# Additive attention masks of the first batch: four 64 by 64 array tiles in place of full matmuls, in an attention and MLP-mixer kernel

## The chip, the cores and the metric

The kernel runs on one core of a Trainium2 chip. The metric is the device time of one execution in microseconds; several executions are timed, and one more is profiled. The core's engines appear in the profile as PE (TensorE; its weight loads are PEld), DVE (VectorE), ACT (ScalarE), POOL (GpSimd) and SP, which here only issues DMAs.

## The reference

Four batches of 768 rows go through windowed attention with sink columns (8 heads of width 64), and the result, 512 wide, through a mixer: a token MLP over the rows, a residual, and a channel MLP with a residual.

```
scores = scale * q @ k.T                      # per batch and head, 768 x 768
keep   = (column < 4) | (0 <= row - column < 128)
a      = softmax(where(keep, scores, -1e9))
x      = a @ v                                # heads side by side: 768 x 512
u      = x + (relu(x.T @ w_tok1) @ w_tok2).T  # w_tok1 768 x 256
out    = u + relu(u @ w_ch1) @ w_ch2          # w_ch1 512 x 1536
```

Only two diagonals of 128 x 128 blocks of the scores matter, and the four sink columns.

## The kernel before

The heads are taken two at a time: 16 pairs, four for each batch, with head i of a pair in rows 64i to 64i+63 of the transposed q and k. The work falls into a first stage and a long rest.

*First attention* (`first_attention`, batch 0, pairs 0 to 3). SP loads q and k of the four pairs in float32 (`load_raw`, line 81); an engine casts each to bf16 (`cast`: ACT for pair 0's q, POOL for pair 3, DVE for the others). `turn` transposes a pair's q or k on TensorE by 64-row halves against `ident` (line 442) and the results are copied out as qT and kT, in two parts each. The scores come in three groups g for each pair: 512, 512 and 384 columns for each head, both heads in one PSUM tile `ps_sc` of two slots, one half of the tile for each head. `scores` (matmuls of 64 rows by 128 columns, the heads in the two row halves) adds to what `masked` has put there: -32768 where a score is masked out. `masked` writes that with a matmul of the identity by the mask, 128 rows by 128 columns, one for each head. ACT then takes the exponential (line 509) straight out of PSUM. Eleven of the twelve groups are masked this way (`MASKED_BY_PE`); the one of pair 3, group 0 is masked by a multiplication on DVE. `score_sinks` does the sink columns for two pairs, `pv` the product with v, with `recip` and `norm` on DVE behind it. The values v come by POOL's DMAs with a cast (`load_v`, line 102), the first four rows of v for the sinks by four small SP loads (line 188) into `v_sink_f`, which DVE has set to zero before, and which POOL casts to `v_sink`. POOL's list has then v of pairs 1 and 2, `w_tok1` (line 127), v of pair 3, and so on.

*The rest*: the token mixing (`mix_h` with w_tok1, `mix_u` with w_tok2), the attention of batches 1 to 3, where no mask is added by TensorE, and the channel MLP (`mix_channels`, lines 849 to 940), which is most of TensorE's work.

*The order.* Until line 200 or so each engine's instructions stand in the order in which the program names them. From there `Plan.run` makes the order: it goes through units of TensorE work and the operations of the other engines behind them, with a cost in nanoseconds for each, and gives the next place to what can begin first by its own reckoning. A unit marked `half` is one that works on 64-row halves; between a `half` unit and another it reckons `SWITCH` (95), and from the first attention's units it prefers one of the same kind. So a unit's cost and its mark change the order of all that comes later, on every engine. The order, once made, is fixed in the program.

At the start of the program DVE has this list: `ones`, zeros in `mask_add`, six memsets of the ones columns of `v_aug` (line 169), zeros in `kTs` (182) and `v_sink_f` (184), four small memsets (192), and then what the plan gives it, the cast of pair 0's k first. POOL makes `ident`, cuts `mask_add` with two affine selects (159, 163) and sets its sink rows to zero (167).

Of the kernel before, what the change touches and what calls it, by code (L numbers as in the profile page):

```python
# [10 lines left out]
BF16 = mybir.dt.bfloat16  # L11
# [5 lines left out]
def kernel(  # L17
# [13 lines left out]
    nc = tc.nc  # L31
    B, H, S, D = q.shape
    P = 128
# [15 lines left out]
    singles = ctx.enter_context(tc.tile_pool(name="singles", bufs=1))  # L49
# [13 lines left out]
    def bank(tag, *shape, dtype=FP32, slot=None):  # L63

        n = given[tag].pop(0) if slot is None else slot
        return psum.tile([P, *shape], dtype, name=f"ps_{tag}", tag=f"{tag}{n}", bufs=1)

    in_order = tc.keep_in_program_order
# [39 lines left out]
    def mm(*args, **kwargs):  # L108
        in_order(nc.tensor.matmul(*args, skip_group_check=True, **kwargs))  # L109
# [19 lines left out]
    done = {}  # L129
# [8 lines left out]
    def keep_warm(n, slot):  # L138
# [12 lines left out]
    mask_add = singles.tile([P, 4, 2, P], BF16)  # L151
    mask_adds = [mask_add[:, ts(n, 2)] for n in range(2)]
    in_order(nc.vector.memset(mask_add, 0.0))
    ident = singles.tile([P, P], BF16)
    in_order(nc.gpsimd.memset(ident, 0.0))
    in_order(nc.gpsimd.affine_select(
        out=ident, in_=ident, compare_op=ALU.not_equal, fill=1.0, base=0, pattern=[[-1, P]], channel_multiplier=1,
    ))
    in_order(nc.gpsimd.affine_select(
        out=mask_add[:, :, 0], in_=mask_add[:, :, 0], compare_op=ALU.is_ge,  # L160
# [3 lines left out]
        out=mask_add[:, :, 1], in_=mask_add[:, :, 1], compare_op=ALU.is_ge,  # L164
        fill=MASKED, base=-1, pattern=[[0, 4], [-1, P]], channel_multiplier=1,
    ))
    in_order(nc.gpsimd.memset(mask_add[0:n_sink, 2], 0.0))
    for n in range(NV):
        in_order(nc.vector.memset(v_buf[n][:, :, :, D:D1], 1.0))

# [14 lines left out]
    for n in range(4):  # L185
        i, odd = n // 2, n % 2
        rows = slice(D * i + ODD * odd, D * i + ODD * odd + n_sink)
        in_order(nc.sync.dma_start(  # L188
            out=v_sink_f[rows, odd::2, i, 0:D],
            in_=v[0].rearrange("(p o i) s d -> i o s p d", i=2, o=2)[i, odd, 0:n_sink],  # L190
# [166 lines left out]
    def unit(ns, fn, deps=(), need=None, then=(), half=False):  # L357

        op = Op({"PE": float(ns)}, fn, deps, then, size=float(ns))
        for f in then:  # L360
            if op not in f.deps:
                f.deps.append(op)
        op.need = need or {}
        op.half = half
        return op
# [102 lines left out]
    def width(g):  # L468
        return 3 * P if g == NT // 2 - 1 else 4 * P

    def masked(p, g):

        def run():
            ps = tiles["ps_s", p, g] = bank("sc", 2, 4 * P)
            for i in range(2):
                mm(
                    ps[:, i, 0:width(g)], ident,
                    mask_adds[g == 0].rearrange("p k n q -> p (k n q)")[:, 0:width(g)], start=True, stop=False,
                )

        x = done["exp", p, g] = Op({}, None)
        deps = [done["tk", 0]] if p == 0 else []
        done["mask", p, g] = unit(width(g) * 0.84, run, deps, {"sc": [[x]]})
        return done["mask", p, g]

    def scores(p, g):
# [295 lines left out]
    def first_attention():  # L782

        for p in range(NHP):
            prepare(p)
        turned = [turn(p, n) for p in range(NHP) for n in range(2)]
        masks, scored, out = [], [], []
        for p in range(NHP):
            for g in range(NT // 2):
                if (p, g) in MASKED_BY_PE:  # L790
                    masks.append(masked(p, g))
                scored.append(burst(scores(p, g)))
                if g == 0 and p == NHP - 1:
                    scored.append(score_sinks(p))
            if p == 1:
                out.append(score_sinks(p))
            if p % 2:
                out += [pv(n, half) for n in (p - 1, p) for half in range(2)]
        tokens = []
        for g in range(2):  # L800
            tokens.append([mix_h(0, g, t, 1) for t in range(NTOK)])
            tokens[g] += [mix_u(0, g, st, 2, g == 0 or st == 2) for st in range(0, NT, 2)]
            tokens[g] += [transpose_u(0, g, st, 2) for st in range(0, NT, 2)]
        return scored, masks, turned, out, *tokens[::-1]
# [265 lines left out]
```

## Time and profile before

| | us |
|---|---|
| median of 3 runs | 209.58 |
| lowest and highest | 209.21, 210.65 |
| the profiled execution's own time | 209.46 |
| its span, first instruction to last | 207.7 |

The span is what the profile's times are counted in; 1.76 us lie around it. The granted clock of TensorE was 0.998 over the span. Busy shares of the span: PE 95%, PEld 57%, DVE 55%, ACT 55%, POOL 32%. A matmul's time in the profile goes from its start to its modelled end, so that one that follows closely on another overlaps it: the distance between starts, not the duration, is what one more matmul costs.

The matmuls of `masked` are the rows `ps_sc<-mask_add,ident`: twelve of 512 and eight of 384 columns were recorded (the program has fourteen and eight), from 6.7 to 20.8 us after the start.

### The profile page before, as it was taken

Reading aid. Unit: us, or ns where it says so; the run is one execution under the profiler, and the core shown is the slowest. Engines: PE = TensorE matmul, PEld = TensorE weight load, DVE = VectorE, ACT = ScalarE, POOL = GpSimd, SP = SyncE. Lnnn points to the kernel's source line nnn. Section 1 sums busy time; section 2 is a strip of 40 time slices with the busy share of each in tenths; the row PEclk is TensorE's granted clock in tenths of the full one; section 3 lists DMA queues with packets and bytes.
Section 4 is the critical chain, followed back from the end, with each engine's and each line's share of the span. In section 5 each row is a group of like instructions: output and inputs, shape, how many; then the busy total and the mean of one; then the engine's idle time right before and its main releaser. Section 6 shows DMA issues by size and latency. Waiting matters only on the chain.

```text
span 207.7 us, 5034 instructions
## 1 busy us (share of the span) xinstructions
PE 198.0 (95%) x2126; PEld 119.3 (57%) x2145; DVE 114.3 (55%) x252; ACT 114.4 (55%) x202; POOL 67.5 (32%) x86
## 2 busy tenths in 40 slices
PE   6699999999999999999999999999999999999994
PEld 2345975566665665557656645666666445665443
DVE  4786664777577675867576552767674421000222
ACT  4799668878727435867684241868751103774000
POOL 6399759794699980720000000000000000000000
PEclk9999999999999999999999999999999999999999
DMA  6999999999999999795000212100001122000222
GB/s 198 283 260 182 172 174 191 156 164 201 156 159 176 185 206 195 52 70 37 3 0 5 101 51 104 51 5 0 3 0 49 56 101 101 3 0 0 101 104 101
DMA packets 73222, 21.57 MB, mean 104 GB/s; under 512 B 63216, under 2 KB 70256, under 8 KB 73200
## 3 DMA queue, kind: packets, MB, share of 16 engines
q0 software_dynamic: 67232, 11.80, 71.9%
q1 hardware_dynamic: 5968, 9.45, 12.9%
q8 instruction: 17, 0.28, 0.6%
q14 instruction: 5, 0.04, 0.1%
HBM read 26.75 MB, written 6.29 MB: 159 GB/s over the span
## 4 chain that ended last, share of the span: by engine, by line
PE 83%; DMA 6%; DVE 4%; ACT 2%; issue 2%; POOL 1%; SPq 0%; POOLq 0%; DVEq 0%
PE ps_mx L109 75%; PE ps_sc L109 5%; DMA w_tok<-in_moe_w_tok_dram 4%; DMA v_sink_f<-in_v_dram 2%; PE ps_sc L460 2%; DVE x_sb L615 1%; ACT qT L116 1%; DVE kT L118 1%; POOL v_aug L102 1%; PE ps_mx L745 1%; ACT v1T L122 1%; DVE recip L612 1%; PE ps_mx L112 1%; POOL v_sink L118 0%; SPq L188 0%
## 5 line engine op out<-in xcount | busy, mean ns | idle before, releaser
L109 PE MATMUL ps_mx<-uT,w_ch 128*128 128x384 bf16 x384 | 68.3, 326 | 0.9 <-DVE x_sb L615 0.9
L109 PE MATMUL ps_mx<-w_ch,v1T 128*128 128x512 bf16 (+2 forms) x299 | 64.2, 362 | 0.9 <-issue 0.3
L122 ACT ACTIVATE v1T<-ps_mx 128x384 bf16<-128x384 f32 x74 | 36.3, 493 | 33.7 <-PE ps_mx L109 22.9
L109 PEld LDWEIGHTS <-w_ch 128*128 128x128 bf16 x384 | 35.5, 98 | 25.0 <-DVE x_sb L615 2.5
L109 PEld LDWEIGHTS <-v1T 128*128 128x128 bf16 x312 | 28.9, 98 | 29.2
L509 ACT ACTIVATE pT<-ps_sc 128x1024 bf16<-128x1024 f32 (+1 forms) x48 | 44.4, 956 | 2.2 <-PE ps_sc L109 1.9
L884 DVE TENSOR_TENSOR o_sb<-ps_mx,u_sb 128x512 f32<-128x512 f32 x23 | 15.9, 691 | 44.6 <-PE ps_mx L109 44.6
L94 POOL DMA_DIRECT2D q_bf<-in_q_dram x24 | 19.7, 822 | 4.7 <-DMA w_ch<-in_moe_w_ch_dram 2.4
L109 PEld LDWEIGHTS <-w_tok 128*128 128x128 bf16 x192 | 18.3, 98 | 4.8 <-DMA w_tok<-in_moe_w_tok_dram 0.5
L94 POOL DMA_DIRECT2D k_bf<-in_k_dram x24 | 19.6, 820 | 3.1 <-DMA w_ch<-in_moe_w_ch_dram 1.7
L102 POOL DMA_DIRECT2D v_aug<-in_v_dram x16 | 16.4, 1028 | 10.9 <-PE ps_mx L109 8.0
L118 DVE COPY kT<-ps_sc 128x768 bf16<-128x768 bf16 x11 | 10.5, 958 | 17.0 <-ACT qT L116 17.0
L516 DVE TENSOR_TENSOR pT<-pT,mask_main 128x1024 bf16<-128x1024 bf16 (+1 forms) x24 | 14.5, 620 | 3.6 <-ACT pT L509 3.5
L109 PE MATMUL ps_sc<-qT,kT 64*128 64x256 bf16 x192 | 15.5, 262 | 0.3
L109 PE MATMUL ps_mx<-v_aug,pT 128*128 128x65 bf16 x352 | 15.3, 194 | 0.0
L716 DVE TENSOR_TENSOR u_sb<-ps_mx,x_sb 128x512 bf16<-128x512 f32 x20 | 12.7, 685 | 4.2 <-PE ps_mx L109 4.2
L109 PEld LDWEIGHTS <-pT 128*128 128x128 bf16 x352 | 13.5, 97 | 2.0 <-issue 0.6
L124 DVE TENSOR_SCALAR v1T<-ps_mx 128x384 bf16<-128x384 f32 x22 | 12.1, 554 | 2.7 <-PE ps_mx L109 2.0
L109 PE MATMUL ps_mx<-h1T,w_tok 128*128 128x256 bf16 x96 | 12.6, 273 | 0.0
L116 ACT ACTIVATE qT<-ps_sc 128x768 bf16<-128x768 bf16 x11 | 8.9, 810 | 6.4 <-PE ps_sc L460 6.2
L109 PE MATMUL ps_mx<-x_sb,w_tok 128*128 128x256 bf16 x96 | 12.0, 273 | 0.1
L615 DVE TENSOR_TENSOR x_sb<-ps_mx,recip 128x384 bf16<-128x384 f32 x22 | 11.4, 551 | 0.1
(72 smaller groups left out, 152.2 us busy)
## 6 DMA issues: line engine op xcount, KB each, us to landing
out_dram<-o_sb SPq DMA_DIRECT2D x23, 256.0 KB, 2.0
v_aug<-in_v_dram POOLq DMA_DIRECT2D x16, 192.0 KB, 6.5
w_ch<-in_moe_w_ch_dram POOLq DMA_DIRECT2D x8, 384.0 KB, 8.9
q_bf<-in_q_dram POOLq DMA_DIRECT2D x24, 96.0 KB, 6.6
k_bf<-in_k_dram POOLq DMA_DIRECT2D x24, 96.0 KB, 5.6
q_f<-in_q_dram SPq DMA_DIRECT2D x4, 384.0 KB, 5.6
k_f<-in_k_dram SPq DMA_DIRECT2D x4, 384.0 KB, 5.9
w_tok<-in_moe_w_tok_dram POOLq DMA_DIRECT2D x2, 384.0 KB, 8.1
```

The costliest lines, as they stand in the source:

```text
L94: in_order(nc.gpsimd.dma_start(out=out[:, h], in_=rows[:, h]))
L102: in_order(nc.gpsimd.dma_start(out=v_aug.rearrange("p i t d -> p (i t) d")[:, :, 0:D], in_=v[b].rearrange("h s d -> (h s) d")[2 * hp * S:2 ...
L109: in_order(nc.tensor.matmul(*args, skip_group_check=True, **kwargs))
L116: in_order(nc.scalar.activation(out, in_, AF.Copy))
L118: in_order({"DVE": nc.vector, "POOL": nc.gpsimd}[e].tensor_copy(out=out, in_=in_))
L122: in_order(nc.scalar.activation(out, in_, AF.Relu))
L124: in_order(nc.vector.tensor_scalar_max(out=out, in0=in_, scalar1=0.0))
L509: in_order(nc.scalar.activation(part(tiles["pT", p][:, :, ds(2 * g, 2)]), tiles["ps_s", p, g][:, :, 0:width(g)], AF.Exp, scale=scale,))
L516: in_order(nc.vector.tensor_tensor(out=pt, in0=pt, in1=m, op=ALU.mult))
L615: in_order(nc.vector.tensor_tensor(out=x_sb[b][:, :, ds((2 * hp + i) * D, D)], in0=tiles["ps_o", p, i][:, :, 0:D], in1=tiles["recip", p, i ...
L716: in_order(nc.vector.tensor_tensor(out=u_part(b, g, s0, n), in0=tiles["ps_u", b, g, s0], in1=x_sb[b][:, s0:s0 + n, c0:c0 + cn], op=ALU.add,))
L884: in_order(nc.vector.tensor_tensor(out=o_sb.rearrange("p (g c) -> p g c", g=2), in1=u_rows(b, st), in0=tiles["ps_out", b, st].rearrange("p ...
```

## The change

A second copy of the additive masks, `mask_swap`, is made by two DVE copies of 64 rows by 1024 columns: the lower 64 rows hold the upper 64 rows of `mask_add` and the other way round. The copies stand in the program right behind the masks' last step and ahead of the memsets of `v_aug`, `kTs` and `v_sink_f`.

`masked` now issues four matmuls for each group in place of two. Each takes 64 rows of a mask and the 64 by 64 corner of the identity that belongs to these rows, and writes 64 partitions of one head's half of `ps_sc`:

| matmul | rows read | mask | partitions written | head's half |
|---|---|---|---|---|
| i=0, x=0 | 0-63 | mask_add | 0-63 | 0 |
| i=0, x=1 | 64-127 | mask_add | 64-127 | 0 |
| i=1, x=0 | 0-63 | mask_swap | 64-127 | 1 |
| i=1, x=1 | 64-127 | mask_swap | 0-63 | 1 |

The unit's reckoned cost goes from 0.84 to 0.44 ns a column, and it gets the mark `half`.

```diff
     in_order(nc.gpsimd.memset(mask_add[0:n_sink, 2], 0.0))
+    mask_swap = singles.tile([P, 4, 2, P], BF16)
+    for x in range(2):
+        in_order(nc.vector.tensor_copy(out=mask_swap[ds(D * x, D)], in_=mask_add[ds(D * (1 - x), D)]))
     for n in range(NV):
         in_order(nc.vector.memset(v_buf[n][:, :, :, D:D1], 1.0))
...
         def run():
             ps = tiles["ps_s", p, g] = bank("sc", 2, 4 * P)
             for i in range(2):
-                mm(
-                    ps[:, i, 0:width(g)], ident,
-                    mask_adds[g == 0].rearrange("p k n q -> p (k n q)")[:, 0:width(g)], start=True, stop=False,
-                )
+                m = (mask_add, mask_swap)[i][:, ts(int(g == 0), 2)].rearrange("p k n q -> p (k n q)")
+                for x in range(2):
+                    rows = ds(D * x, D)
+                    mm(
+                        ps[ds(D * (x ^ i), D), i, 0:width(g)], ident[rows, rows], m[rows, 0:width(g)],
+                        start=True, stop=False,
+                    )
 
         x = done["exp", p, g] = Op({}, None)
         deps = [done["tk", 0]] if p == 0 else []
-        done["mask", p, g] = unit(width(g) * 0.84, run, deps, {"sc": [[x]]})
+        done["mask", p, g] = unit(width(g) * 0.44, run, deps, {"sc": [[x]]}, half=True)
```

In the order that the plan makes of it, every engine's list differs from about the first scores on: in the first stage ACT gets two pairs of the small kTs copies in place of two kT copies, and DVE the other way round; the mask and scores of pair 3, group 1 stand ahead of the first `mix_h`. SP's and POOL's lists keep their order.

## The prediction

> **What bounds the kernel now.** I read the page's slices first, then the chain that ended last, then the waits and the timeline of the first 28 us, the only stretch with the lines that the diff touches.
>
> ```profile
> PE   6699999999999999999999999999999999999994
> ...
> ACT  4799668878727435867684241868751103774000
> ...
> DMA  6999999999999999795000212100001122000222
> ...
> PE 83%; DMA 6%; DVE 4%; ACT 2%; issue 2%; POOL 1%; SPq 0%; POOLq 0%; DVEq 0%
> ```
>
> A slice is 5.2 us. After the first two or three, TensorE is full to the end: a microsecond taken off the start should come off the whole. The chain says what the start is made of:
>
> ```profile
> 2.58 0.50 DVE v_sink_f L184
> ...
> 4.12 4.17 DMA v_sink_f<-in_v_dram
> ...
> 8.46 0.92 POOL v_sink L118
> 9.38 1.95 POOL v_aug L102 x2
> 11.33 7.89 DMA w_tok<-in_moe_w_tok_dram
> ...
> 19.27 0.83 PE ps_mx L109 x6
> 20.10 1.25 PE ps_sc L109 x12
> 21.34 5.84 PE ps_mx L109 x88
> ```
>
> Up to 19.27 us the chain is no mask at all: a DVE memset, four tiny loads of the sink rows, a cast and two loads on POOL, and the landing of w_tok1, which TensorE's first token-mixing matmul waits for. From there TensorE itself carries it. The masks' part in it is within "ps_sc x12" at 20.10.
>
> Beside that chain, ScalarE was full from 8 to 20 us. The waits of the first 30 us (engine, line, releaser, total, times, longest) hold two waits of its exponentials:
>
> ```profile
> ACT pT L509 <- PE ps_sc L109: 1.1, 2, 0.7
> ...
> PE ps_sc L109 <- ACT pT L509: 0.9, 2, 0.5
> ```
>
> ```profile
> 10.00:15.00 5.00, 4.53 (x74) 2.32 (x72) 4.36 (x11) 4.97 (x9) 5.00 (x7) 1.00 1.73 278
> 15.00:20.00 5.00, 4.69 (x78) 2.94 (x80) 3.42 (x10) 4.78 (x8) 5.00 (x7) 1.00 1.65 186
> ```
>
> Columns after the length: busy PE, weight loads, DVE, ACT, POOL, then granted clock (1.00), DMA, GB/s. From 10 to 20 us ACT is at 9.75 of 10, PE at 9.2. So a shorter mask there mostly buys TensorE time to wait for ScalarE. The two places where TensorE kept ScalarE waiting are here (start, length, engine, line):
>
> ```profile
> 5.78 0.56 DVE L118 CAST k_bf<-k_f 128x768 bf16<-128x768 f32 x1 [2.29 <-DMA k_f<-in_k_dram]
> ...
> 6.68 1.04 PE L109 MATMUL ps_sc<-mask_add,ident 128*128 128x512 bf16 x4
> 6.78 0.87 ACT L116 ACTIVATE kT<-ps_mx 128x384 bf16<-128x384 bf16 x2 [0.62 <-PE ps_mx L442]
> ...
> 7.65 0.61 PE L109 MATMUL ps_sc<-qT,kT 64*128 64x256 bf16 x8
> ...
> 8.08 1.02 ACT L509 ACTIVATE pT<-ps_sc 128x1024 bf16<-128x1024 f32 x1 [0.43 <-PE ps_sc L109]
> ```
>
> ```profile
> 19.93 0.92 PE L109 MATMUL ps_sc<-mask_add,ident 128*128 128x512 bf16 x4
> ...
> 21.22 1.73 ACT L509 ACTIVATE pT<-ps_sc 128x1024 bf16<-128x1024 f32 x2 [0.66 <-PE ps_sc L109]
> ```
>
> At 6.68 four masks stand ahead of the first scores; the first half of kT is out at about 7.27 (half of 0.87 after 6.78, and 0.05), the scores begin at 7.65. At 19.93 four more stand ahead of the last two score groups.
>
> **The change, part by part.** *Masks.* Eleven groups, 7 of 512 columns and 4 of 384. Four 512 masks took 1.04 us, of which about 0.17 is the tail of the last (a lone one is 0.38): 0.216 each, so 0.162 for 384. Before: 14 x 0.216 + 8 x 0.162 = 4.3 us. After there are 44 matmuls of 64 rows by 64 columns. No row shows such tiles. Nearest are the scores, 64 rows by 128 columns: 8 of 256 in 0.61 us is (0.61 - 0.17)/4 = 0.11 for two, what one would cost alone, so two row halves do run together. From below: all four run together, 2.2 us, a saving of 2.15. From above: one after the other, 8.6 us, a loss of 4.3. I take four together, since the scores show row halves doing just that, and their heads, like here, write different banks.
>
> *Where that lies.* The first two groups: 0.43 instead of 0.86, so the scores wait for kT at 7.3 and the first exponential starts at 7.75 instead of 8.08: -0.33 on ScalarE's row. The middle seven (2.7 us before) lie beside ScalarE: nothing on the path. The last ones: in the changed kernel's instruction order group 1 of pair 3, its mask and its four scores (0.21), now stands ahead of the first token-mixing matmul, where TensorE idles for w_tok1; behind it only the 384 mask is left. Behind w_tok1's landing there were 0.43 + 0.32 of masks and 0.21 of those scores; now there is 0.16: -0.80 us.
>
> *Mode changes.* Going from 128-row matmuls to 64-row ones costs a gap: the two 512 masks that start at 11.74 have streamed by 12.17 and the 64-row transposes start at 12.27, 0.10 us. Counted in the order up to the scores after the last mask, row changes go from 19 to 14; if 64 by 64 against 64 by 128 is a change as well, to 30. After w_tok1 there were two and there are four or, without the column kind, three or four: +0.1 to +0.2, I take +0.15. [...]
>
> *The copies.* Two DVE copies of 64x1024 bf16 stand ahead of the six v_aug memsets, kTs, v_sink_f and the four small ones, and wait for POOL's second affine select (2.60 + 0.63 = 3.23) and its memset of the sink rows (3.29 + 0.30 = 3.59). A TENSOR_SCALAR of 512 bf16 on DVE took 0.288, two in a row 0.49, so a copy costs between 0.29 and, by the 0.56 of the 768-wide CAST scaled up, 0.75; I take 0.43, between one and two of the TENSOR_SCALARs, the nearest type. The memsets took from 1.95 to 3.49, 1.54. DVE is through at 3.29 + 0.86 + 1.54 = 5.69 (5.4 to 6.3), and its next work, the k cast, began at 5.78 when its data came: 0 to 0.55 late, I take +0.1. That cast is at the head of ScalarE's row, so it comes off the 0.33. The four mask_main and mask_first operations behind it had room up to the 7.67 cast.
>
> *The sink chain.* v_sink_f's memset ends at 5.28 instead of 3.08, and the SP queue holds four sink loads, then q and k of pairs 2 and 3, behind it. The last sink load is issued near 6.3. From above it needs the 4.17 us that it had: +2.2 on w_tok1. From below nothing: SP's first four loads landed in order (the casts that waited for the first two start at 3.84 and 5.78, SP's own waits for the other two end at 7.22 and 8.34) and the sink rows at 8.29 with the fourth, so they had been standing behind it. A 256 KB store lands in a median of 2.0 us, 6.3 + 2.0 = 8.3: I take +0.2, and w_tok1 lands at 19.4. SP's next four loads were issued at 4.47, 5.77, 7.22 and 8.34. The first two now go at about 6.6 and 7.0, still before the fourth load has landed and its queue runs dry, so I cost them nothing; without that cover they come 2.1 and 1.2 us later, and cost ScalarE up to 1 us near 12.
>
> *Other engines.* ScalarE's list up to its last exponential loses two 0.50 kT copies and gains two pairs of 4-column kTs copies (two of ScalarE's 4x65 copies are 0.51): nothing. DVE gains two kT copies of 0.55 and loses two kTs pairs of 0.3: +0.5 in a stretch where it had 2.2 of 10 us free.
>
> *Sum.* TensorE behind w_tok1: -0.80 + 0.15 + 0.2 = -0.45. ScalarE's row: -0.33 + 0.1 - 0.66 (the wait at 21.22) = -0.9, so it doesn't hold TensorE up. The later order differs little: the transposes of u and the first channel matmuls near 29 us are split otherwise, around a wait for DVE (0.70 at 29.42 in the chain), which can get shorter or longer by some 0.4; I take 0. In all -0.45. The profiled execution took 209.46 (span 207.7 and 1.76 around it; 0.12 under the median 209.58): **209.0 us**.
>
> **The rivals.**
> 1. *The change buys nothing:* tiles run two at a time, a group costs 0.43 as before, the mode changes and copies stay. Then the first exponential is no earlier, the last group gains only by its new place: 0.96 less the 0.32 of its mask, so -0.64 + 0.15 + 0.2 = -0.3, and up to +0.5 from the later k cast and the mode changes before: 209.2 to 209.7, say 209.5. For it: no row shows column halves together. Against: the heads and the column halves are disjoint.
> 2. *Slower, the tiles serialise:* two row halves write one bank (on different partitions), which no row of before does, and the four run one by one. First scores at 6.68 + 8 x 0.216 + 0.1 = 8.5, +0.86; the middle seven +2.7 against some 0.8 of idle TensorE, +1.9; the last +0.3: +3.1, so **212.5 us**. It decides from a group of about 0.75 us on. [...]
> 3. *Slower, the sink chain:* the loads keep their 4.17 us, w_tok1 lands at 21.4 with TensorE idle from 19.3: +2.2 - 0.65 = +1.55, **211.0 us**. Decides from a landing later than about 9.1 us.
> 4. *A luckier order:* waits after 30 us (1.6 us of TensorE in all) go too: 209.0 - 1.6 = 207.4. For it: the order there changes. Against: each wait is under 0.5 and has its own cause.
>
> **How the numbers follow.** Forecast 0.55 (its own range 208.3 to 209.6), rival 1 0.17, rival 2 0.09, rival 3 0.13, rival 4 0.06. Later units are reordered, which I take as 0.5 us either way. The range of 8 in 10 leaves out rival 2, half of rival 4 and the far end of 3: 207.8 to 211.0. About 1% (2.1 us) is what a measurement of this kernel can tell from no change: faster than 207.5 needs rival 4, 0.06; slower than 211.7 is rival 2 and the worst of 3, 0.11; within, 0.83.
>
> **What would show it.** A 512 group as four MATMULs with starts close together and the next scores some 0.3 us behind; first exponential near 7.85; v_sink's cast near 8.7 and token mixing near 19.4; the exponential at 21.22 without its 0.66 wait. It is wrong if a group takes 0.4 or more, if the k cast starts after 6.2, or if w_tok1 lands after 20.

## The result and the profile after

| | before | after |
|---|---|---|
| median of 13 runs each, us | 209.69 | 211.27 |
| lowest and highest, us | 209.21, 210.65 | 210.42, 212.42 |
| the profiled execution, us | 209.46 | 211.39 |
| its span, us | 207.7 | 209.6 |

The ratio is 1.0067 (95% interval 1.005 to 1.0084): 1.4 us slower by it (the medians lie 1.6 apart), where 0.45 us less was forecast (209.0, range 207.8 to 211.0). It lies within the 1%, on the other side of zero, and the time is above the range. A ratio leaves out an execution over 1.5% above the quickest of its kernel; below, that is one, in experiment 5.

The page's slices of the changed kernel, and its chain's shares:

```profile
PE   6698999999999999999999999999999999999994
...
ACT  4878768978928425869494150879661102774000
...
PEclk9759999999999999999999999999999999999999
DMA  6999999999999999495000212100000222000222
...
PE 88%; DVE 5%; ACT 3%; issue 2%; POOL 1%; POOLq 0%; DVEq 0%; ACTq 0%
```

TensorE is full from the fourth slice on, as before. Two things are new: DMA has gone from 6% of the chain to nothing, DVE and ACT from 6% together to 8%; and in the second and third slice the granted clock is .7 and .5. The chain of waits that ends near 30 us begins like this (start, length, what):

```profile
2.65 0.60 POOL mask_add L163
3.27 0.61 DVE mask_swap L170
3.89 0.42 DVE mask_swap L170
...
4.40 0.34 DVE v_aug L172 x6
4.74 0.25 DVE kTs L185
...
5.05 0.50 DVE v_sink_f L187
...
5.98 0.57 DVE k_bf L118
...
6.60 0.35 PE ps_mx L445 x12
...
23.86 5.47 PE ps_mx L109 x77
```

Before, this chain went over the sink rows and the landing of w_tok1. Now it goes over the copies and DVE's memsets to the cast of k. The timeline of the same stretch:

```profile
3.27 1.04 DVE L170 COPY mask_swap<-mask_add 64x1024 bf16<-64x1024 bf16 x2 [1.33 <-POOL mask_add L163]
...
4.78 1.14 POOL L102 DMA_DIRECT2D v_aug<-in_v_dram  x1 [1.19 <-DVE v_aug L172]
...
5.57 1.32 SPq L191 DMA_DIRECT2D v_sink_f<-in_v_dram  x4
...
6.88 0.40 PE L109 MATMUL ps_sc<-mask_add,ident 64*64 64x512 bf16 x2
6.88 0.40 PE L109 MATMUL ps_sc<-mask_swap,ident 64*64 64x512 bf16 x2
6.93 0.39 SPq L81 DMA_DIRECT2D q_f<-in_q_dram  x1
...
7.12 0.38 PE L109 MATMUL ps_sc<-mask_add,ident 64*64 64x512 bf16 x2
7.12 0.38 PE L109 MATMUL ps_sc<-mask_swap,ident 64*64 64x512 bf16 x2
...
7.53 0.71 PE L109 MATMUL ps_sc<-qT,kT 64*128 64x256 bf16 x8
...
7.96 1.94 ACT L516 ACTIVATE pT<-ps_sc 128x1024 bf16<-128x1024 f32 x2
```

Read the mask rows first: all four matmuls of a group start within a hundredth of a microsecond (6.88 and 6.88), and the next group starts 0.24 us later, where two full masks took 0.43. The tiles run four together. But the first exponential starts only 0.12 us earlier (7.96 for 8.08), and above it stand the delays. v's first load is issued at 4.78 (3.55 before), the sink loads at 5.57 (3.10), the q of pair 2 behind them at 6.93 (4.47). What comes of these is here:

```profile
9.85 0.61 POOL L118 CAST v_sink<-v_sink_f 128x520 bf16<-128x520 f32 x1 [3.93 <-DMA v_sink_f<-in_v_dram]
...
12.83 0.80 DVE L118 CAST q_bf<-q_f 128x768 bf16<-128x768 f32 x1 [1.46 <-DMA q_f<-in_q_dram]
...
14.93 0.83 POOL L118 CAST q_bf<-q_f 128x768 bf16<-128x768 f32 x1 [0.66 <-DMA q_f<-in_q_dram]
...
18.19 1.94 ACT L516 ACTIVATE pT<-ps_sc 128x1024 bf16<-128x1024 f32 x2 [0.52 <-PE ps_mx L109]
...
22.00 0.83 PE L109 MATMUL ps_mx<-x_sb,w_tok 128*128 128x256 bf16 x6
```

The cast of pair 2's q, at 10.79 before, waits 1.46 us for its data and starts at 12.83. Token mixing starts at 22.00 (19.27 before) and waits for no weights: TensorE was at work on scores until then. From there on nothing more is lost. The first matmul of `mix_u` starts at 25.89 (23.75 before), 2.14 us later; from it to the end of the span the changed kernel needs 183.7 us, the one before 184.0. So all of it happens in the first 26 us. Windows of the kernel before, and then of the changed one (columns as in the prediction: length, busy PE, PEld, DVE, ACT, POOL, granted clock, DMA, GB/s):

```profile
6.00:8.00 2.00, 1.60 (x24) 0.85 (x24) 1.80 (x8) 1.03 (x3) 0.00 (x0) 1.00 1.52 275
8.00:10.00 2.00, 1.45 (x36) 0.71 (x30) 1.39 (x4) 1.92 (x3) 1.54 (x2) 1.00 1.39 292
```

```profile
6.00:8.00 2.00, 1.38 (x28) 0.68 (x28) 1.80 (x8) 1.03 (x4) 0.00 (x0) 1.00 1.48 199
8.00:10.00 2.00, 1.71 (x32) 1.04 (x30) 1.45 (x3) 2.00 (x3) 0.15 (x1) 0.50 1.08 170
...
14.00:16.00 2.00, 1.72 (x36) 0.80 (x30) 1.42 (x3) 1.42 (x3) 1.34 (x3) 0.79 2.28 167
```

From 6 to 10 us the core moved 199 and 170 GB/s, before 275 and 292: loads that used to run here had not been issued. And from 8 to 14.8 us TensorE ran at half clock, which the profile of before doesn't show. That is not in every execution: four of the 13 had a mean clock of .983 or .984 and took 211.39 to 211.66; five of the others took 210.42 to 210.59, and four 211.1 to 212.4 at 1.0. (One of the five, 210.47, had .992.) So the halved clock belongs to this profile, and even the quickest executions are 0.7 us above before's median.

### The profile page after: what moved, and what is told of

Its sections match the earlier page's. It is cut to its first block, busy times and chain, and to the rows that moved or that the text cites. A ratio compares the mean times of both kernels' runs of the same rounds, so it can differ in the third digit from the quotient of the medians.

```text
span 209.6 us, 5101 instructions
## 1 busy us (share of the span) xinstructions
PE 201.3 (96%) x2167; PEld 119.9 (57%) x2167; DVE 114.8 (55%) x251; ACT 115.0 (55%) x205; POOL 67.2 (32%) x86
## 2 busy tenths in 40 slices
DMA packets 73222, 21.57 MB, mean 103 GB/s; under 512 B 63216, under 2 KB 70256, under 8 KB 73200
## 4 chain that ended last, share of the span: by engine, by line
PE 88%; DVE 5%; ACT 3%; issue 2%; POOL 1%; POOLq 0%; DVEq 0%; ACTq 0%
PE ps_mx L109 76%; PE ps_sc L109 8%; PE ps_sc L463 2%; ACT pT L516 1%; DVE x_sb L622 1%; DVE kT L118 1%; ACT qT L116 1%; PE ps_mx L445 1%; PE ps_mx L752 1%; ACT v1T L122 1%; DVE recip L619 1%; DVE mask_swap L170 0%; PE ps_mx L112 0%; DVE u_sb L723 0%; POOL mask_add L159 0%
## 5 line engine op out<-in xcount | busy, mean ns | idle before, releaser
L109 PE MATMUL ps_mx<-w_ch,v1T 128*128 128x512 bf16 (+2 forms) x312 | 65.7, 363 | 0.0
L109 PE MATMUL ps_sc<-qT,kT 64*128 64x256 bf16 x192 | 16.4, 272 | 0.1
L109 PEld LDWEIGHTS <-kT 64*128 64x128 bf16 x192 | 6.8, 95 | 8.2 <-issue 5.9
```

## The experiments

Theories: (P) the place of the copies, on DVE ahead of the memsets that hold back loads; (O) the new order that comes of the unit's cost and its mark; (C) the clock. Against these stands (T), that the tiles themselves cost time. Every ratio is to the kernel before, timed beside the other on the same chip.

**1. The copies later.** The changed kernel, with the copies behind the small memsets of `v_sink_f`.

```diff
-    mask_swap = ...; both copies      # behind mask_add's last step
     ...
         in_order(nc.vector.memset(v_sink_f[rows, odd::2, i, D:D1], 1.0))
+    mask_swap = ...; both copies
```

> The changed kernel with the two mask_swap copies moved behind the memsets of v_aug, kTs and v_sink_f on DVE. Position theory (the loss is made by the copies' place: the SP loads behind v_sink_f go 2.4 us late and pair 2's q lands at 12.8 instead of 10.8): SP's loads go out as before, pair 2's q cast starts near 10.8, time 208.8 to 209.4. Tile and order theory (64 by 64 tiles or the new order cost TensorE): 210.4 and more at full clock, as in the changed kernel. Clock theory (shorter masks leave TensorE too little to do before 8 us, so its clock is halved for 6.8 us whatever DVE does): clock 0.5 from 8 us in most executions, 210 to 210.6.

Measured: 210.75 us (209.54 to 211.25), ratio 1.0037 (1.0016 to 1.0058). SP's loads are issued at 3.10, 4.59 and 5.37 again and pair 2's q is cast at 11.35. That takes back about 0.3 of the 0.67%; the intervals overlap, so the next run is needed beside it. Something besides the place is left. The halved clock is still there, too: three of the nine executions had a mean of .983 or .984 (211.01 to 211.25) and one .992, so late loads aren't what it needs.

**2. The copies alone.** The kernel before with the two copies in the change's place; nothing reads them.

```diff
     in_order(nc.gpsimd.memset(mask_add[0:n_sink, 2], 0.0))
+    mask_swap = singles.tile([P, 4, 2, P], BF16)
+    for x in range(2):
+        in_order(nc.vector.tensor_copy(out=mask_swap[ds(D * x, D)], in_=mask_add[ds(D * (1 - x), D)]))
```

> The kernel before with nothing but the two mask_swap copies, in the place that the change gives them; the masks are written by full matmuls as before and nobody reads the copies. Position theory: slower by what the late loads cost, 210.3 to 211, with the wait of DVE for pair 2's q as in the changed kernel. Tile and order theory: 209.5 to 209.9, as before. Clock theory: as before as long as the clock stays full; a halved clock here would say that late loads alone bring it about.

Measured: 210.98 us (210.62 to 211.27), ratio 1.0053 (1.0035 to 1.0071), with before's matmuls and order. Its timeline has the changed kernel's late issues, and something else:

```profile
4.78 1.14 POOL L102 DMA_DIRECT2D v_aug<-in_v_dram  x1 [1.18 <-DVE v_aug L172]
5.57 1.32 SPq L191 DMA_DIRECT2D v_sink_f<-in_v_dram  x4
6.93 0.40 SPq L81 DMA_DIRECT2D q_f<-in_q_dram  x1
...
7.03 1.89 PE L109 MATMUL ps_sc<-mask_add,ident 128*128 128x512 bf16 x4
...
9.50 1.02 ACT L512 ACTIVATE pT<-ps_sc 128x1024 bf16<-128x1024 f32 x1 [1.50 <-PE ps_sc L109]
...
12.53 0.88 DVE L118 CAST q_bf<-q_f 128x768 bf16<-128x768 f32 x1 [0.35 <-DMA q_f<-in_q_dram]
```

Two copies that no one uses cost 1.1 us: that P costs is shown, and as a large part of the whole. That it costs by the late loads is not shown by this run. Pair 2's q is waited for by 0.35 us only, and from the first exponential to 20 us ScalarE has no wait over 0.2 us. What is late in this profile is the first exponential, 9.50 for 8.08, and it waited 1.50 us for TensorE: the four masks took 1.89 us, before 1.04. TensorE was at about half speed, though the clock column says 1.00: twelve transposes took 0.53 us at 9.68 and then 0.35 at 10.99; in the profile of before they took 0.50 at 4.78 and 0.35 from 6.40 on. One profile can't tell whether the copies bring that about or this execution happened to have it. Two of the six executions (210.82 and 211.17) had a mean clock of .992, with full matmuls for the masks.

**3. The order alone.** The kernel before, masks in full matmuls, with the unit's new cost and mark.

```diff
-        done["mask", p, g] = unit(width(g) * 0.84, run, deps, {"sc": [[x]]})
+        done["mask", p, g] = unit(width(g) * 0.44, run, deps, {"sc": [[x]]}, half=True)
```

> The kernel before with only the mask unit's reckoned cost (0.44) and its half mark changed: full matmuls, no copies, but an order much like the changed kernel's. Position theory: within 0.4 of before, 209.3 to 210.1. Order theory: slower, 210.3 and more. Clock theory: as before, clock full.

Measured: 210.36 us (209.49 to 211.37), ratio 1.0036 (1.0017 to 1.0055). TensorE's work is the same; the order is another, and with it which of ACT and DVE makes some of the small copies. It costs 0.75 us. Its timeline says where:

```profile
14.14 0.84 POOL L118 CAST q_bf<-q_f 128x768 bf16<-128x768 f32 x1
...
15.04 0.35 PE L442 MATMUL ps_mx<-ident,q_bf 64*128 64x64 bf16 x12
...
15.32 0.36 PE L109 MATMUL ps_mx<-v_aug,pT 128*128 128x65 bf16 x6
...
16.49 1.94 ACT L509 ACTIVATE pT<-ps_sc 128x1024 bf16<-128x1024 f32 x2 [0.52 <-PE ps_mx L109]
```

Pair 3's q transposes, which wait for POOL's cast (through at 14.98), stand on TensorE ahead of pair 0's product with v; before, they came behind the first of it. Pair 2's exponential writes the buffer that pair 0's product reads (`pT` has two), and so waits 0.52 us for that product.

**4. Warm matmuls.** The changed kernel with five matmuls of `ones`, 512 columns each, ahead of the transposes of pair 0's k, where TensorE idles for the cast.

```diff
         def run():
+            if p == 0 and n == 1:
+                keep_warm(5, given["mx"][0])
             ps = [bank("mx", NT, D, dtype=BF16) for _ in range(2)]
```

> The changed kernel with five 512-column matmuls of ones between the transposes of pair 0's q and k, where TensorE waits for data (extra work whose result nobody reads). Clock theory: the clock is full in all executions and the time the least that the changed kernel shows, 210.4, or better. Position theory: no better than 210.4, pair 2's q still lands near 12.8. If the clock still halves, it is not the idle time before 6.6 us that sets it.

Measured: 210.72 us (210.01 to 211.54), ratio 1.005 (1.0025 to 1.0075). No execution of the seven had the halved clock, and most of the loss is still there. By the two ratios the five matmuls bring 0.2%, within their intervals. In this profile the clock column is 1.00 in every stretch of 2 us up to 32, and it shows what the late loads cost (SP's issues are as late as in the change):

```profile
13.08 0.56 DVE L118 CAST q_bf<-q_f 128x768 bf16<-128x768 f32 x1 [2.19 <-DMA q_f<-in_q_dram]
...
14.14 0.49 ACT L116 ACTIVATE qT<-ps_mx 128x384 bf16<-128x384 bf16 x1 [0.98 <-PE ps_mx L447]
```

DVE waits 2.19 us for pair 2's q, and ScalarE 0.98 us for what TensorE makes of it.

**5. The tiles in the old order.** Copies late (as in 1), tiles, but cost 0.84 and no mark.

```diff
-        done["mask", p, g] = unit(width(g) * 0.44, run, deps, {"sc": [[x]]}, half=True)
+        done["mask", p, g] = unit(width(g) * 0.84, run, deps, {"sc": [[x]]})
```

> The four-tile masks with the copies moved behind the memsets, and the mask unit reckoned as before the change (0.84, no half mark), so that every engine's order is that of the kernel before. Order theory (what is left of the loss with the copies moved is the new order): 209.0 to 209.8 where the clock is full, and the exponential of pair 2, group 0 no longer waits for the product with v of pair 0. Tile theory (64 by 64 tiles themselves cost, by their changes of mode): 210.3 and more. Clock theory: the masks ahead of 8 us are as short as in the changed kernel, so the clock halves in some executions, about 1 us dearer.

Measured: 210.0 us (209.38 to 214.23), ratio 1.0006 (0.9984 to 1.0027). With place and order undone the loss is gone: T falls. So is any gain. Three of the twelve executions had a mean clock of .984 and one .992.

**6 and 7. A third pT buffer**, on the order alone (3) and on the late copies (1).

```diff
-                tiles["pT", p] = pt_pool.tile([P, 2, NT, 2, P], BF16, name="pT")
+                tiles["pT", p] = pt_pool.tile([P, 2, NT, 2, P], BF16, name="pT", bufs=3)
```

> The kernel before with the changed mask unit's cost and half mark alone, as in plan_alone, and three buffers for pT in place of two: the order of every engine is that of plan_alone, but the exponentials of pair 2 need not wait for the product with v of pair 0. Wait theory (the new order puts pair 3's q transposes, which wait for POOL's cast, ahead of pair 0's product with v, and ScalarE waits behind both): ScalarE's waits at 14 to 17 us go, 209.3 to 209.9. If the order costs in another way: 210.2 to 210.6, as plan_alone.

> The changed kernel with the copies moved behind the memsets and three buffers for pT; order as in copies_late. Wait theory: 208.9 to 209.5 at full clock, 1 us more where the clock halves. Otherwise as copies_late, 210.0 to 210.8.

Measured: 210.11 us, ratio 1.0007 (0.9991 to 1.0022), for 1.0036 with two buffers; and 210.47 us, 1.0017 (0.9997 to 1.0037), for 1.0037. The order of 6 is that of 3, and the wait has gone:

```profile
15.95 0.36 PE L109 MATMUL ps_mx<-v_aug,pT 128*128 128x65 bf16 x6
...
16.50 1.93 ACT L509 ACTIVATE pT<-ps_sc 128x1024 bf16<-128x1024 f32 x2
```

The exponential now runs beside pair 0's product with v, of which the last matmuls start after 16.7. It starts no earlier than in 3 (16.49), since here the first exponential came 0.63 us later (7.93 for 7.30). Both pairs move by 0.2 to 0.3% the same way; each by itself is hardly more than its intervals. Beside these the kernel before took 209.88, 0.2 more than beside 3. With that, 6 is at the upper end of what was expected if the wait is the cost, and 7 is within what was expected if it is not (210.0 to 210.8). So what the wait is worth isn't settled. The third buffer in the kernel before wasn't run, so it may give a little there as well.

**8 and 9. Warm matmuls in the old order**, with the tiles (5 and 4 together) and in the kernel before.

> As tiles_old_plan, with five 512-column matmuls of ones between the transposes of pair 0's q and k (extra work whose result nobody reads). Clock theory: the clock is full in every execution, and the time is the lower end of what tiles_old_plan shows, 209.0 to 209.6. If the clock is full in tiles_old_plan too, both are the same.

> The kernel before with nothing but the five 512-column matmuls of ones between the transposes of pair 0's q and k (extra work whose result nobody reads). If these matmuls bring something of themselves, 209.3 or less; if they only keep the clock up where it would halve, which the kernel before never showed, the time of before, 209.5 to 209.9, and the lower time of tiles_old_warm is the tiles' own.

Measured: with the tiles 209.55 us (208.85 to 210.03), ratio 0.9984 (0.9968 to 1.0); without them 210.22 us (209.84 to 210.59), 1.0008 (0.9988 to 1.0027). The first is the best version, about 0.3 us below before, at the edge of what its interval can tell from nothing. The two differ by 0.24%, 0.5 us, which is the best figure here for the tiles' own worth; the intervals overlap. Its start is instructive:

```profile
5.21 1.99 PE L109 MATMUL ps_mx<-ones 128*128 128x512 bf16 x5
...
7.26 0.35 PE L447 MATMUL ps_mx<-ident,k_bf 64*128 64x64 bf16 x12
...
8.61 1.02 ACT L518 ACTIVATE pT<-ps_sc 128x1024 bf16<-128x1024 f32 x1
```

The five matmuls push the transposes of k from 6.40 to 7.26 and the first exponential from 8.08 to 8.61, and `mix_u` still starts at 23.87 (23.75 before). So half a microsecond at the head of ScalarE's row is slack here, or the shorter masks behind it make it good; this run doesn't part the two. One of its twelve executions had a mean clock of .992.

**10. Only SP's loads late.** The kernel before with the unused copies between the memsets of `kTs` and `v_sink_f`, behind those of `v_aug`.

```diff
     in_order(nc.vector.memset(kTs0, 0.0))
+    mask_swap = ...; both copies, read by nothing
     v_sink_f = singles.tile([P, NHP, 2, D1], FP32)
```

> The kernel before with the two copies between the memsets of kTs and v_sink_f, unused by anyone: v's first load goes out on time, SP's sink loads and its loads of pairs 2 and 3 as late as in the changed kernel, k's first cast 0.2 late. If SP's late loads are what the copies cost: 210.5 to 211, as copies_alone, with pair 2's q cast after 12.5. If the late load of v was: 209.5 to 209.9.

Measured: 210.51 us (209.87 to 211.27), ratio 1.0023 (1.0002 to 1.0043).

```profile
3.55 1.39 POOL L102 DMA_DIRECT2D v_aug<-in_v_dram  x1
4.99 1.32 SPq L191 DMA_DIRECT2D v_sink_f<-in_v_dram  x4
...
6.64 1.89 PE L109 MATMUL ps_sc<-mask_add,ident 128*128 128x512 bf16 x4
...
9.11 1.02 ACT L512 ACTIVATE pT<-ps_sc 128x1024 bf16<-128x1024 f32 x1 [1.50 <-PE ps_sc L109]
...
11.82 0.56 DVE L118 CAST q_bf<-q_f 128x768 bf16<-128x768 f32 x1
```

v's load is on time, SP's are 1.9 us late, and the time lost is about half of what the copies cost in 2; the two intervals overlap. The kernel before took 210.07 beside this run, 0.4 more than beside 2; with that the time lies between the two expectations, and the sign of late loads of SP, a cast of pair 2's q after 12.5, did not come: the cast is at 11.82, and it waits for nothing. As in 2, the delay of this profile is in the first exponential, behind masks at half speed (1.89 us for four). So the split between v's load, SP's and the clock isn't settled.

**11. Tiles two at a time.** Warm matmuls and old order as in 8, no copies: both heads read `mask_add` and keep to the tiles that need no exchange of rows, so that the two heads' tiles are the same two of the four.

```diff
+                m = mask_add[:, ts(int(g == 0), 2)].rearrange("p k n q -> p (k n q)")
+                for x in range(2):
+                    rows = ds(D * x, D)
+                    mm(ps[ds(D * x, D), i, 0:width(g)], ident[rows, rows], m[rows, 0:width(g)], start=True, stop=False)
```

> No second mask copy: four 64 by 64 matmuls a group, but both heads on the same two tiles of the array (rows and columns 0 to 63, rows and columns 64 to 127), order of the kernel before, and the five matmuls of ones. A group takes 0.43, as full matmuls do, since only two tiles run together. If half the mask time is worth what tiles_old_warm showed: 209.6 to 209.9; if the first stage is bound by loads and ScalarE whatever a mask costs: the same as tiles_old_warm, 209.4 to 209.6.

Measured: 210.61 us (209.86 to 211.09), ratio 1.0024 (1.0006 to 1.0042).

```profile
7.80 1.05 PE L109 MATMUL ps_sc<-mask_add,ident 64*64 64x512 bf16 x8
```

Eight matmuls, two groups, in 1.05 us, as long as four full ones before (1.04): two at a time, 0.22 for each two. Against 8 that is 0.4% more, with no copies to pay for; against 9, whose masks take as long, 0.16%, within the intervals. Both expectations were lower, also with the 0.4 us that before took more beside this one. The copy is what lets all four run together (0.24 us a group in the change).

**12. Copies late, new order, warm matmuls.** The edits of 1 and 4 together.

> The changed kernel with the copies moved behind the memsets and the five matmuls of ones: new order, tiles, and a clock kept up. Clock theory: never halved, and 0.3 to 0.5 below copies_late's median, 210.2 to 210.5. Order theory: still above the kernel before by what plan_alone lost, less what the tiles bring, 209.9 to 210.5.

Measured: 210.28 us (209.69 to 211.4), ratio 1.0019 (0.9998 to 1.004). Three of the 12 executions had a mean clock of .991 or .992, the profiled one (211.4) at half clock for about 3.4 us, by its column (.97 from 8 to 12 us, .60 from 12 to 16). So the warm matmuls don't keep the clock up in every case.

## Why the prediction was wrong

Two things that the forecast put at nothing cost time: the place of the copies, and the new order. Taken from experiments 2, 3 and 8 less 9, the parts are +1.1 us for the copies' place (0.53%), +0.75 for the order (0.36%) and -0.5 for the tiles (0.24%): +1.35, against 1.4 measured. Each has an interval of some 0.4 to 0.5 us either way, and that the sum agrees so well is luck. By the same parts experiment 1, order and tiles, should lose 0.12%, and it lost 0.37 (0.16 to 0.58). Undone one after the other in the changed kernel, the place gives back 0.30% (the change less 1), the order 0.31% (1 less 5), and the tiles are left with 0.06% (5). So the place cost 0.6 to 1.1 us, the order 0.65 to 0.75, and the tiles save between nothing and, with the warm matmuls, 0.5.

That 0.5 has the size of the forecast's -0.45, by luck: the forecast made it behind w_tok1's landing, most of it by the new place of pair 3's group, which the old order of experiment 8 doesn't have. In 8's profile `mix_u` starts no earlier than before, so where the tiles save isn't seen.

*Right.* The four tiles run together (0.24 us a group; rival 2 reckoned on 0.86, and two at a time, rival 1, is what experiment 11 shows when the exchange is left out). On rival 2's doubt: two row halves wrote one head's half of `ps_sc` side by side, on different partitions (both at 6.88), without holding each other up. The k cast is 0.2 late (0.1 taken). Nothing is lost after 30 us: TensorE's waits are 1.1 us there (1.6 before).

*The copies' duration.* 0.61 and 0.42, 1.04 together, for 0.86 forecast; within the bounds, and 0.2 us of the delay.

*"SP's next four loads … I cost them nothing": the first step that failed.* The bound beside it, 2.1 us later, is what came: pair 2's q was cast 2.04 us later, after a wait of 1.46 us for its data, and in experiment 4, with the clock column at 1.00, DVE waited 2.19 us and ScalarE behind it 0.98, the bound's "up to 1 us". My cover was that the queue still held older loads; but the rate fell to 170 GB/s at 8 to 10 us, and it had been 292. That the queue was not empty at the moment of issue didn't make the issue free. How much of the 0.6 to 1.1 us is theirs stays open: the profiles of 2 and 10, with SP's issues late too, lost most of their time ahead of the first exponential, to a slow TensorE.

*A wait I did not see.* The copies also stand ahead of the memsets of `v_aug`, which hold back v's first load on POOL by 1.2 us. I counted those memsets as DVE's time and did not ask who waits for them. A cost of it isn't shown: the load landed at 10.61, before at 10.87.

*The sink chain.* v_sink is cast 1.4 us later, not 0.2; the last sink load landed at 9.69, 2.8 us after its issue was through (6.89), neither the old 4.17 nor the 2.0 taken. Yet w_tok1, issued 1.1 us later (12.42 for 11.33), isn't what the token mixing waits for, since scores stand before it until 22 us. So rival 3 came near the measured time, 211.0, by another path, not by w_tok1: in its stead the trace has waits for pair 2's and 3's data and for the pT buffer.

*"Other engines … nothing", and the later order at 0: the second step that failed.* The order has a term of 0.75 us by itself. I compared how many operations each engine had up to a point and not who waits for whom: pair 3's transposes, held by POOL's cast, in front of pair 0's product, and pair 2's exponential behind that.

*ScalarE's row at -0.9.* The first exponential came 0.12 earlier, not 0.23, and it bought nothing to be seen: experiment 8 has it 0.5 later than before and `mix_u` only 0.12. The waits inside the row grew instead: 0.52 for the pT buffer, and for the transposes of q and k 1.4 and 0.9 us in the first 30 us, where they were 0.6 and 0.6. The chain goes over the row's exponentials (7.96, 15.07 and 18.19), so it did hold TensorE up.

*The mode changes.* The sum doesn't need the 0.15 us; no run took them apart. Of the change between 64 by 64 and 64 by 128 that it reckons with, no row of before shows a cost; the changed kernel's trace has 0.10 us there: the masks at 21.33 have streamed by 21.57 (0.24 a group), and the scores start at 21.67.

*Not in it at all: the clock.* The halved clock took about 1.1 us in four executions of 13 (211.39 to 211.66, against 210.42 to 210.59 of the five quickest). The price of a mask, 0.216 us, was read at full speed, from four masks at 6.68 that took 1.04; in the profile of experiment 2 four masks took 1.89 us. The five warm matmuls lower the ratio by 0.17, 0.18 and 0.22% in the three versions with four tiles (4 against the change, 12 against 1, 8 against 5) and raise that of before by 0.08. Each is within its intervals; together they make the clock a rival worth some 0.2 to 0.3% of the tiles' versions, 0.4 to 0.6 us, that no run rules out.

## What to carry to other kernels

A short operation at the head of an engine's list costs what it delays (1.1 us for two copies of 1.04 together that nothing read, experiment 2): for each instruction behind it, ask which DMA waits for it and which loads stand behind that DMA in its queue. Where an order is planned from costs, a changed cost or mark is a change of its own (0.75 us, experiment 3): run it alone, with the old instructions, and look for a unit that waits for a late engine in front of one that frees a buffer. And a gain counts only where the row that it shortens sets the end; push that row's start later by as much, and see whether the time moves (a first exponential 0.53 us later moved `mix_u` by 0.12, experiment 8). Before two profiles are compared, see how long a matmul of the same shape took in the same stretch of each (four masks: 1.04 us before, 1.89 in experiment 2).

## What the hardware showed that I had not expected

*The clock column said 1.00 while TensorE was slow.* In the tiles' version of experiment 8 a matmul of 512 columns took 0.63 us at 4.00 (a lone mask at full speed 0.38), with the column at 1.00, and twelve transposes took 0.50 at 4.78 and 0.35 at 7.26. In that of experiment 2 four masks at 7.03 took 1.89 us with the column at 1.00, and the transposes came to 0.35 at 10.99. The twelve transposes of k, at 6 to 7 us, took 0.35 before and in the changed kernel, 0.50 in experiments 2 and 10. I take that for some of the scatter of a microsecond in every comparison here; how much of it, no run shows.

*How long the clock was halved.* It was 0.50 for 6.83 us in the changed kernel's profile, from 8.01 to 14.84, and for about 3.4 us in experiment 12's, half as long. TensorE was busy for 1.4 of the 2 us ahead of the fall. Before, with 1.6 of 2, none of 35 executions had a mean under .998. By an estimate from the spans a mean of .992 fits a fall of 3.4 us and .984 one of 6.8. By these means most falls are in versions with tiles, but two of six executions of experiment 2 have one with full masks, and warm matmuls (8 and 12) don't rule it out. What sets it off stays open.

*Four 64 by 64 tiles stream at nearly the rate of one full matmul* (0.216 us for 512 columns, in the prediction): 0.24 us for a group of 512 columns (starts at 6.88 and 7.12), and two heads whose tiles are the same two take 0.45 (experiment 11).
